# A slot table for two attention layers: transposes and maxima moved in front of the value sums, the turning of sums one slot later

## The chip, the cores and the metric

The kernel runs on one core of one Trainium2 chip. The metric is the device time of one execution in microseconds (us), lower is better. A core has five engines with queues of their own: TensorE (PE in the profile; PEld is its loading of weights), VectorE (DVE), ScalarE (ACT), GpSimd (POOL) and SyncE (SP, which only issues DMAs here). Each engine takes its own instructions in order and waits on semaphores for the others.

## What is computed

Four layers follow each other, A, B, A, B, on 2048 rows of 512 numbers; each layer normalises its input and adds its output to it. A is a linear attention. B, which the change touches, is a causal softmax attention inside four segments of 512 rows, with 32 heads of width 16, plus a memory that carries sums of keys and values from segment to segment:

```python
def _B_ref(x, wq, wk, wv, wo, beta):
    ...
    for s in range(N):
        qs, ks, vs = q[:, :, s], k[:, :, s], v[:, :, s]
        logits = jnp.einsum("bhqd,bhkd->bhqk", qs, ks) * scale + mask
        p = _softmax(logits, axis=-1)
        a_dot = jnp.einsum("bhqk,bhkd->bhqd", p, vs)
        pq = phi(qs)
        num = jnp.einsum("bhld,bhde->bhle", pq, M)
        den = jnp.einsum("bhld,bhd->bhl", pq, z)[..., None] + 1e-6
        a_mem = num / den
        o = g * a_mem + (1.0 - g) * a_dot
        outs.append(o)
        pk = phi(ks)
        M = M + jnp.einsum("bhld,bhle->bhde", pk, vs)
        z = z + jnp.einsum("bhld->bhd", pk)
    o = (lambda x, *d: x.transpose(*d))(jnp.stack(outs, 2).reshape(B, H, S, Dh), 0, 2, 1, 3).reshape(B, S, D)
    return o @ wo

x = A_x
x = x + _A_ref(_layernorm(x, axis=-1), A_wqkv, A_w_phi, A_wo)
x = x + _B_ref(_layernorm(x, axis=-1), B_wq, B_wk, B_wv, B_wo, B_beta)
x = x + _A_ref(_layernorm(x, axis=-1), A_wqkv, A_w_phi, A_wo)
x = x + _B_ref(_layernorm(x, axis=-1), B_wq, B_wk, B_wv, B_wo, B_beta)
```

## The kernel before

**Groups, rows and slots.** A layer B is 4 segments (s) of 8 groups (m counts all 32); a group is four heads. `LayerB.steps` (L1381) walks through slots k; R = 5 slots make a *row*, and row n of a segment holds the softmax of one group. In this document "slot 0" to "slot 4" are the five slots of a row (k % 5), and row 0 to row 7 the eight rows of a segment. Each layer has 160 such slots, after a lead-in of 25.

**What a slot issues, in this order** (L1470 to L1506): the group's logits and their exponentials (`attend`, L1193: TensorE writes tile `lg`, ScalarE takes the exponential into `P`, GpSimd cuts the diagonal blocks); one of five steps of the maxima of a later group (`maxima`, L1148: logits once more, into a pair of PSUM banks, and VectorE takes row maxima of them, the `top` operations, into `mxs`); work that was put off from earlier slots; `stack` (L1137: three DMAs on SP that put the split queries or keys, tile `ta`, into the stacked set `e`, when k % 5 is in `STACK`); the words of the slot's cell in the table that begin with `<`; in slot 0 the value sums of the group before (`weighted`, L1235: `P` times `v`, then ScalarE copies the sums to `U`); and then the other words of the cell.

**The order is fixed.** Every matmul and transpose passes through `held` (L165), and the other engines through `Ordered` (L145): each instruction of an engine stands behind the one before it in program order. So the table decides what each engine does next.

**The words** (`do`, L1395): `Q`, `V`, `O`, `P` with a number of steps are projections (TensorE, accumulating in `g` banks over four slots of a row); `a` is half of a memory read (`reads`, L1091); `t` and `m` are the two halves of a memory write (`writes`, L1106: `t` transposes keys on TensorE and ScalarE copies them to `KN`, `m` multiplies them with `v` and VectorE and GpSimd update the memory); `ln` is the transposing step of a later segment's normalisation (`columns`, L386: TensorE transposes, ScalarE writes `hh`, VectorE the rest `hl`), `n` and `N` are its earlier steps; `turn` (L1296) prepares the output rows of the segment before (with TensorE transposes only in the first segment, where the rows are those of layer A); `max` is `put_maxima` (L1184); `fin` is `finish` (L1261: VectorE turns `U` over, divides, and GpSimd adds to `ot`); `cv` is `convert` (L1286: VectorE turns finished sums `ot` for the output projection).

**PSUM.** Eight banks: two for `lg`, one each for `mx` and `my`, four for `g`. The maxima use `mx` and `my`, or two `g` banks where k % 5 is in `SPARE` (2, 4). `put_maxima` also uses `mx`:

```python
# maxima, L1172
if self.k % R in SPARE if self.k >= 0 else self.k % 2:
    pb = [PS("g", G) for _ in range(2)]
else:
    pb = [PS(t, 1) for t in ("mx", "my")]
# put_maxima, L1187
pt = PS("mx", 1)
tp(pt[0:16, 0:P], self.mx.pop(m), ident)
mt = T2("mt", MT, F32R, shape=(16, P))
act.activation(mt, pt[0:16, 0:P], AF.Copy, scale=-1.0)
```

`PS("mx", 1)` asks for a tile in the one buffer of that name; a new tile there waits until the tile before it has been read. The five steps of the maxima differ in width: in one step each bank takes 128 and 384 columns (twice, for two halves of the heads), in two steps 512, in one 256 twice.

**Lead.** The maxima of group m run in slots 5m - `LEAD` to 5m - `LEAD` + 4, and `max` in slot 0 of row n takes group n + 1. With `LEAD` = 9 the last of the five steps falls into that same slot 0.

**Projections to stacks.** `proj_pair` (L1035) ends in slot 4 of a row; `projected` (L1058) copies the result to `raw`, and in the next row splits it into `ta` (high part on ScalarE, low part on GpSimd): the queries in slot 1, the keys in slot 2. `stack` in row n takes group n + 3. The pairs stand in rows 0, 1, 4 and 6, so that three of the eight groups are stacked in the row in which they are split: those of rows 1, 5 and 7.

## Time and profile before

| | before |
|---|---|
| median of 3 runs | 1359.47 us (1357.38 to 1362.27) |
| the profiled execution, own time | 1360.54 us |
| its span, first to last instruction | 1358.8 us |
| mean granted TensorE clock | 0.994 |
| VectorE busy | 1045.2 us (77%) |
| ScalarE busy | 841.5 us (62%) |
| GpSimd busy | 751.4 us (55%) |

The first layer B lies at about 286 to 690 us of the span, the second at about 950 to 1340 us. A row takes some 12 to 13.5 us there. Busy TensorE time is modelled: a matmul's row in the trace runs from its start to the end of its drain, so that neighbouring rows overlap, and a wait shorter than the drain shows as no idle time of PE, but as idle time of PEld, which normally runs about a matmul ahead.

### The profile page before, as it was taken

The page shows a single profiled execution, that of the slowest core. Times are in us where ns is not written, and L with a number is a line of the kernel's source. Part 1 is how long each engine was busy: PE and PEld are TensorE (multiplying, and loading weights), DVE is VectorE, ACT ScalarE, POOL GpSimd, SP SyncE. Part 2 cuts the span into 40 slices and gives each one's busy share as a digit, 9 for nine tenths or more (in the row PEclk, how much of TensorE's full clock was granted, in tenths as well). Part 3 has the DMA queues.
Part 4 walks back from the last instruction along what each step waited for, and adds up shares of the span by engine and source line. Part 5 has one row for each costly group of instructions (what it writes and reads, how often), then busy time and mean ns, then how long its engine had stood idle before and what let it go on. Part 6 is the DMA issues. An engine that isn't in the chain of part 4 may idle for free.

```text
span 1358.8 us, 41839 instructions
## 1 busy us (share of the span) xinstructions
PE 1295.2 (95%) x16552; PEld 990.1 (73%) x16552; DVE 1045.2 (77%) x3247; ACT 841.5 (62%) x1274; POOL 751.4 (55%) x1116
## 2 busy tenths in 40 slices
PE   7999989999999999999999998999999999999987
PEld 6887868777767767767668886786777777777665
DVE  4766778778888888887767676787778789788785
ACT  5556345647777777676644433454677867867654
POOL 1668766225558668556324455551456667666552
PEclk9999999999999999999999998999999999999999
DMA  6398437534554545546350103745456454444432
GB/s 205 102 339 264 159 129 232 176 104 133 168 168 137 152 120 139 149 123 182 99 192 22 60 32 126 230 156 151 138 155 178 139 148 124 138 138 104 111 88 79
DMA packets 134419, 196.58 MB, mean 145 GB/s; under 512 B 15440, under 2 KB 61648, under 8 KB 133456
## 3 DMA queue, kind: packets, MB, share of 16 engines
q1 hardware_dynamic: 132256, 193.27, 47.5%
q8 instruction: 131, 2.15, 0.7%
q10 hardware_dynamic: 1968, 0.64, 0.2%
q14 instruction: 64, 0.52, 0.1%
HBM read 101.05 MB, written 39.85 MB: 104 GB/s over the span
## 4 chain that ended last, share of the span: by engine, by line
PE 67%; DVE 14%; ACT 8%; POOL 4%; issue 3%; DMA 2%; SPq 1%; DVEq 0%; ACTq 0%; POOLq 0%
PE g L177 52%; PE lg L177 6%; ACT P L155 4%; PE mx L177 3%; PE g L181 3%; DVE U L155 2%; PE lg L181 2%; DVE g L155 2%; POOL P L155 1%; POOL tb L155 1%; ACT ta L155 1%; DVE mx L155 1%; DVE es L155 1%; PE my L177 1%; DVE hl L155 1%
## 5 line engine op out<-in xcount | busy, mean ns | idle before, releaser
L155 ACT ACTIVATE P<-lg 128x1024 f32<-128x1024 f32 x316 | 324.3, 1026 | 126.1 <-PE lg L177 104.6
L155 POOL TENSOR_SCALAR_AFFINE_SELECT P<-P 128x256 f32<-128x256 f32 (+1 forms) x448 | 191.3, 442 | 197.2 <-ACT P L155 194.6
L155 DVE CUSTOM_DVE_ANT_0 g<-g,mask 128x256 f32<-128x256 f32 (+3 forms) x392 | 190.6, 542 | 17.9 <-PE g L177 17.8
L177 PE MATMUL g<-hh,wqk 64*128 64x512 f32 (+1 forms) x960 | 182.3, 394 | 1.6 <-SPq L155 0.7
L155 DVE CUSTOM_DVE_ANT_0 mx<-mx,mask 128x512 f32<-128x512 f32 (+2 forms) x316 | 158.4, 501 | 24.3 <-PE my L177 22.3
L177 PE MATMUL g<-w,oh 64*128 64x512 f32 (+2 forms) x848 | 170.8, 382 | 2.6 <-ACT oh L155 2.6
L177 PE MATMUL lg<-e,e 64*128 64x512 f32 (+1 forms) x1010 | 151.3, 345 | 13.2 <-ACT P L155 12.6
L155 DVE CUSTOM_DVE_ANT_0 my<-my,mask 128x512 f32<-128x512 f32 (+2 forms) x316 | 163.8, 518 | 0.0
L177 PE MATMUL g<-P,v 128*32 128x128 f32 (+3 forms) x2064 | 152.7, 434 | 1.2 <-DVE mxs L155 0.9
L177 PE MATMUL g<-w,hh 64*128 64x512 f32 (+1 forms) x672 | 143.2, 395 | 2.2 <-ACT w L155 1.3
L155 DVE DVE_READ_ACCUMULATOR2_ANT mxs<- 128x1 f32 x1024 | 144.0, 141 | 0.0
L177 PEld LDWEIGHTS lg<-e,e 64*128 64x128 f32 x1010 | 96.5, 185 | 54.1 <-ACT P L155 31.6
L177 PEld LDWEIGHTS g<-w,oh 64*128 64x128 f32 (+1 forms) x848 | 103.8, 187 | 16.8 <-ACT oh L155 3.5
L177 PEld LDWEIGHTS g<-hh,wqk 64*128 64x128 f32 (+1 forms) x960 | 98.4, 185 | 20.9 <-ACT hh L155 2.0
L177 PE MATMUL g<-w,ol 64*128 64x512 f32 (+2 forms) x424 | 112.1, 377 | 0.5 <-DVE ol L155 0.5
L177 PEld LDWEIGHTS g<-P,v 128*32 128x32 f32 x2064 | 64.1, 110 | 66.1 <-issue 49.1
L177 PE MATMUL g<-hl,wqk 64*128 64x512 f32 (+1 forms) x480 | 101.4, 392 | 2.1 <-DVE hl L155 2.1
L155 ACT COPY tb<-g 128x512 f32<-128x512 f32 (+1 forms) x132 | 70.9, 574 | 45.9 <-PE g L177 44.1
L177 PEld LDWEIGHTS g<-w,hh 64*128 64x128 f32 (+1 forms) x672 | 83.8, 188 | 16.4 <-ACT w L155 1.6
L177 PE MATMUL mx<-e,e 63*128 63x384 f32 (+3 forms) x323 | 89.7, 340 | 6.3 <-ACT mt L155 4.7
L155 POOL TENSOR_TENSOR ot<-ot,wt 128x256 f32<-128x256 f32 x46 | 33.9, 738 | 101.8 <-DVE wt L155 101.8
L177 PE MATMUL g<-w,hl 64*128 64x512 f32 (+1 forms) x336 | 89.4, 393 | 0.0
(164 smaller groups left out, 2987.1 us busy)
## 6 DMA issues: line engine op xcount, KB each, us to landing
e<-ta SPq DMA_DIRECT2D x384, 128.0 KB
wqk<-wqk SPq DMA_DIRECT2D x128, 256.0 KB
x<-x SPq DMA_DIRECT2D x48, 256.0 KB
pq<-tb SPq DMA_DIRECT2D x24, 256.0 KB
tb<-pq SPq DMA_DIRECT2D x24, 256.0 KB
x<-xr SPq DMA_DIRECT2D x22, 256.0 KB
xr<-x SPq DMA_DIRECT2D x20, 256.0 KB
x<-in SPq DMA_DIRECT2D x16, 256.0 KB
```

Of the source, the lines that this page charges most:

```text
L155: i = f(*a, **k)
L177: return held(nc.tensor.matmul(*a, **k))
L181: return held(nc.tensor.transpose(*a))
```

## The change

Only the constants and the four tables change; no function does. `max`, `turn`, `t` and `ln` get a `<` and so stand in front of the value sums of slot 0, and in front of `a`, which had one already; `m` comes a row sooner where it followed `t` by a row, behind the sums; `fin` moves from slot 0 to slot 1 (except in row 6 of `LAST` and `FINAL`), and some `cv` move by one or two slots. `LEAD` = 10 lets the five steps of the maxima run in slots 0 to 4 of one row, and `STACK` = (1, 3) puts the stacking DMAs a slot sooner.

```diff
-STACK = (2, 4)
+STACK = (1, 3)
 SPARE = (2, 4)
...
-LEAD = 9
+LEAD = 10
...
 FIRST = """
-0.0 max v3 fin | 0.1 Q2/6           | 0.2 Q2/6          | 0.3 Q2/6 | 0.4 Q2/6
-1.0 max t0 turn fin | 1.1 Q3/6      | 1.2 Q3/6          | 1.3 Q3/6 | 1.4 Q3/6
-2.0 m0 max turn t1 fin ln | 2.1 O/6 | 2.2 O/6           | 2.3 O/6 | 2.4 O/6
-3.0 m1 max turn turn fin ln | 3.1 O/6 | 3.2 O/6         | 3.3 O/6 | 3.4 O/6
-4.0 max ln ln fin | 4.1 Q0+/6 cv0   | 4.2 Q0+/6         | 4.3 Q0+/6 cv1 | 4.4 load Q0+/6
-5.0 max t2 fin | 5.1 V+/6           | 5.2 V+/6 n        | 5.3 V+/6 n | 5.4 V+/6 w
-6.0 m2 max t3 fin | 6.1 Q1+/6 cv2   | 6.2 Q1+/6 n       | 6.3 Q1+/6 n | 6.4 Q1+/6 w
-7.0 <a0+ m3 max fin | 7.1 V+/6 w | 7.2 V+/6 n        | 7.3 V+/6 n | 7.4 V+/6 w
+0.0 <max v3 | 0.1 Q2/6              | 0.2 Q2/6          | 0.3 Q2/6 | 0.4 Q2/6
+1.0 <t0 <turn <max m0 | 1.1 fin Q3/6 | 1.2 Q3/6         | 1.3 Q3/6 | 1.4 Q3/6
+2.0 <ln <t1 <turn <max m1 | 2.1 fin O/6 | 2.2 O/6       | 2.3 O/6 | 2.4 O/6
+3.0 <ln <turn <turn <max | 3.1 fin O/6 | 3.2 O/6        | 3.3 O/6 | 3.4 O/6
+4.0 <ln <ln <max | 4.1 fin Q0+/6    | 4.2 Q0+/6 cv0     | 4.3 Q0+/6 cv1 | 4.4 load Q0+/6
+5.0 <t2 <max m2 | 5.1 fin V+/6      | 5.2 V+/6 n        | 5.3 V+/6 n | 5.4 V+/6 w
+6.0 <t3 <max m3 | 6.1 fin Q1+/6     | 6.2 Q1+/6 n       | 6.3 Q1+/6 n cv2 | 6.4 Q1+/6 w
+7.0 <max <a0+ | 7.1 fin V+/6 w      | 7.2 V+/6 n        | 7.3 V+/6 n | 7.4 V+/6 w
 """
 GAPS = """
-0.0 <a0 max fin | 0.1 Q2/6 n cv3    | 0.2 Q2/6 n        | 0.3 Q2/6 n | 0.4 Q2/6
-1.0 <a1 max t0 turn fin | 1.1 Q3/6      | 1.2 Q3/6 n        | 1.3 Q3/6 | 1.4 Q3/6
-2.0 <a1 m0 max turn t1 fin ln | 2.1 O/6    | 2.2 O/6           | 2.3 O/6 | 2.4 O/6
-3.0 <a2 m1 max turn turn fin ln | 3.1 O/6  | 3.2 O/6           | 3.3 O/6 | 3.4 O/6
-4.0 <a2 max ln ln fin | 4.1 Q0+/6 cv0  | 4.2 Q0+/6       | 4.3 Q0+/6 cv1 | 4.4 load begin Q0+/6
-5.0 <a3 max t2 fin | 5.1 V+/6 | 5.2 V+/6 n N      | 5.3 V+/6 n N | 5.4 V+/6
-6.0 <a3 m2 max t3 fin | 6.1 Q1+/6 cv2   | 6.2 Q1+/6 n N     | 6.3 Q1+/6 n N | 6.4 Q1+/6
-7.0 <a0+ m3 max fin | 7.1 V+/6      | 7.2 V+/6 n N      | 7.3 V+/6 n N | 7.4 V+/6
+0.0 <max <a0 | 0.1 fin Q2/6 n       | 0.2 Q2/6 n        | 0.3 Q2/6 n cv3 | 0.4 Q2/6
+1.0 <t0 <turn <max <a1 m0 | 1.1 fin Q3/6 | 1.2 Q3/6 n   | 1.3 Q3/6 | 1.4 Q3/6
+2.0 <ln <t1 <turn <max <a1 m1 | 2.1 fin O/6 | 2.2 O/6   | 2.3 O/6 | 2.4 O/6
+3.0 <ln <turn <turn <max <a2 | 3.1 fin O/6 | 3.2 O/6    | 3.3 O/6 | 3.4 O/6
+4.0 <ln <ln <max <a2 | 4.1 fin Q0+/6 | 4.2 Q0+/6 cv0    | 4.3 Q0+/6 cv1 | 4.4 load begin Q0+/6
+5.0 <t2 <max <a3 m2 | 5.1 fin V+/6 | 5.2 V+/6 n N       | 5.3 V+/6 n N | 5.4 V+/6
+6.0 <t3 <max <a3 m3 | 6.1 fin Q1+/6 | 6.2 Q1+/6 n N     | 6.3 Q1+/6 n N cv2 | 6.4 Q1+/6
+7.0 <max <a0+ | 7.1 fin V+/6      | 7.2 V+/6 n N        | 7.3 V+/6 n N | 7.4 V+/6
 """
 LAST = """
-0.0 <a0 max fin | 0.1 Q2/6 n cv3    | 0.2 Q2/6 n        | 0.3 Q2/6 n | 0.4 Q2/6
...
-6.0 <a3 max fin pre | 6.1 cv2         | 6.2 P/4           | 6.3 P/9 | 6.4 P/5 v/1
-7.0 max fin | 7.1 P/4           | 7.2 P/5 v/1       | 7.3 P/4 v/1 | 7.4 P/5 v/2
+0.0 <max <a0 | 0.1 fin Q2/6 n       | 0.2 Q2/6 n        | 0.3 Q2/6 n cv3 | 0.4 Q2/6
+1.0 <turn <max <a1 | 1.1 fin Q3/6   | 1.2 Q3/6 n        | 1.3 Q3/6 | 1.4 Q3/6
+2.0 <ln <turn <max <a1 | 2.1 fin O/6 | 2.2 O/6          | 2.3 O/6 | 2.4 O/6
+3.0 <ln <turn <turn <max <a2 | 3.1 fin O/6 | 3.2 O/6    | 3.3 O/6 | 3.4 O/6
+4.0 <ln <ln <max <a2 | 4.1 fin v/2  | 4.2 v/2 cv0       | 4.3 v/2 cv1 | 4.4 v/2
+5.0 <max <a3 | 5.1 fin v/2          | 5.2 v/2           | 5.3 v/2 | 5.4 v/2
+6.0 <max <a3 fin pre | 6.1 cv2      | 6.2 P/4           | 6.3 P/9 | 6.4 P/5 v/1
+7.0 <max | 7.1 fin P/4              | 7.2 P/5 v/1       | 7.3 P/4 v/1 | 7.4 P/5 v/2
 """
 FINAL = """
-0.0 <a0 max fin | 0.1 Q2/6 cv3      | 0.2 Q2/6          | 0.3 Q2/6 | 0.4 Q2/6
...
-4.0 <a2 max turn turn fin | 4.1 O/6 cv1    | 4.2 O/6           | 4.3 O/6 | 4.4 O/6
...
+0.0 <max <a0 | 0.1 fin Q2/6         | 0.2 Q2/6          | 0.3 Q2/6 cv3 | 0.4 Q2/6
+1.0 <turn <turn <max <a1 | 1.1 fin Q3/6 | 1.2 Q3/6      | 1.3 Q3/6 | 1.4 Q3/6
+2.0 <max <a1 | 2.1 fin O/6          | 2.2 O/6 cv0       | 2.3 O/6 | 2.4 O/6
+3.0 <max <a2 | 3.1 fin O/6          | 3.2 O/6           | 3.3 O/6 | 3.4 O/6
+4.0 <turn <turn <max <a2 | 4.1 fin O/6 | 4.2 O/6        | 4.3 O/6 cv1 | 4.4 O/6
+5.0 <max <a3 | 5.1 fin O/6          | 5.2 O/6           | 5.3 O/6 | 5.4 O/6
+6.0 <max <a3 fin pre | 6.1 cv2      | 6.2 P/4           | 6.3 P/9 | 6.4 P/5
+7.0 <max | 7.1 fin P/4              | 7.2 P/5           | 7.3 P/4 | 7.4
 """
```

`FIRST` is the table of segment 0, `GAPS` of segments 1 and 2; segment 3 uses `LAST` in the first layer B and `FINAL` in the second.

## The prediction

> **What bounds the kernel now.** First the page's busy times, then a window in the first layer B (columns: us, then busy us and instructions of PE, PEld, DVE, ACT, POOL, the granted clock, DMA share, GB/s).

> ```profile
> PE 1295.2 (95%) x16552; PEld 990.1 (73%) x16552; DVE 1045.2 (77%) x3247; ACT 841.5 (62%) x1274; POOL 751.4 (55%) x1116
> ```

> ```profile
> 400.00:450.00 50.00, 48.71 (x752) 36.55 (x744) 40.38 (x150) 37.24 (x57) 34.33 (x52) 1.00 0.47 131
> ```

> TensorE is the bound, in the middle of layer B too: 48.7 of 50 us, with VectorE at 40.4 close behind. What a reordering can win is only what TensorE waits. The waits of its weight loads tell more than those of its matmuls, whose drains hide short stalls:

> ```profile
> PEld lg L177 <- ACT P L155: 31.6, 54, 1.8
> PEld g L177 <- DVE mxs L155: 22.9, 51, 1.3
> ...
> PEld mx L177 <- ACT mt L155: 13.6, 33, 0.6
> PEld g L177 <- POOL P L155: 13.1, 41, 0.8
> PEld g L177 <- DVE hl L155: 9.7, 14, 0.9
> ```

> Columns: total us, times, longest. Loads run about 0.2 us ahead (one weight load takes 0.19), so I count each such wait less 0.2 us as lost time.

> Now one slot 0 (a row 1 of `GAPS`) on TensorE, from the timeline:

> ```profile
> 411.45 0.39 PE L177 MATMUL lg<-e,e 64*128 64x512 f32 x2
> 411.68 0.39 PE L177 MATMUL mx<-e,e 63*128 63x512 f32 x1
> 412.00 0.77 PE L177 MATMUL g<-mem,tb 128*32 128x34 f32 x64
> 412.69 2.36 PE L177 MATMUL g<-P,v 128*32 128x512 f32 x32
> ...
> 415.27 0.28 PE L181 MATMUL mx<-ident,mxs 128*16 128x128 f32 x1
> 415.39 0.60 PE L181 MATMUL g<-ident,tb 128*128 128x128 f32 x4
> 415.82 0.60 PE L181 MATMUL g<-ident,x 128*128 128x128 f32 x4
> 416.35 0.50 PE L177 MATMUL lg<-e,e 64*128 64x512 f32 x2
> ```

> Logits, the maxima's products into mx and my, memory read (0.7 us), value sums, and only then, 3.6 us after the products, the turning of the maxima into the same bank mx. By then VectorE has long read mx, so this turning waits for nothing. That distance is what the change takes away.

> **The turned maxima, moved forward.** After it, slot 0 puts the 128- and 384-column step into mx and my, and `max` asks for bank mx with at most some transposes between. How long mx stays taken is seen where the same step stands today, in a slot 3:

> ```profile
> 407.44 0.28 PE L177 MATMUL mx<-e,e 63*128 63x256 f32 x1
> ...
> 407.73 0.40 PE L177 MATMUL g<-hh,wqk 64*128 64x512 f32 x2
> ...
> 407.93 0.30 DVE L155 CUSTOM_DVE_ANT_0 mx<-mx,mask 128x128 f32<-128x128 f32 x1 [0.33 <-PE my L177]
> ...
> 408.14 0.14 DVE L155 DVE_READ_ACCUMULATOR2_ANT mxs<- 128x1 f32 x1
> ...
> 408.91 0.14 DVE L155 DVE_READ_ACCUMULATOR2_ANT mxs<- 128x1 f32 x1
> ...
> 409.42 0.14 DVE L155 DVE_READ_ACCUMULATOR2_ANT mxs<- 128x1 f32 x1
> ```

> The third read, the last of mx, ends at 409.05, 1.61 us after the products began. TensorE learns of such an end 0.10 us later (below, 411.76 + 0.14 to 412.00). Its next work started 0.29 us after the products. So the wait is 1.61 + 0.10 - 0.29 = 1.42 us, less what stands between. A block of four transposes covers 0.43 us (415.39 to 415.82).

> ```profile
> 411.76 0.14 DVE L155 DVE_READ_ACCUMULATOR2_ANT mxs<- 128x1 f32 x1
> 412.00 0.66 PEld L177 LDWEIGHTS g<-mem,tb 128*32 128x32 f32 x64 [0.36 <-DVE mxs L155]
> ```

> So a row costs 1.42, 0.99, 0.56 or 0.13 us with 0, 1, 2 or 3 blocks in front of `max`. Blocks per row, from the tables: `GAPS` 0,1,2,1,2,1,1,0: 2 x 1.42 + 4 x 0.99 + 2 x 0.56 = 7.9 us, four such segments 31.7. `FIRST` (its `turn` transposes too) 0,2,3,3,2,1,1,0: 2 x 1.42 + 2 x 0.99 + 2 x 0.56 + 2 x 0.13 = 6.2, twice 12.4. `LAST` 0,0,1,1,2,0 in rows 0 to 5 (row 6 has no maxima beside it): 6.8. `FINAL` has none: 6 x 1.42 = 8.5. **Sum +59 us** in 60 rows. Behind the waiting turn stand, on TensorE, the read, the value sums and all later slots; nothing can pass it. Bounds: if the turn waited only for its own 128 columns (first read, ending at 408.28), a bare row costs 0.84 + 0.10 - 0.29 = 0.65, a row with one block 0.22, others nothing: 2 x 0.65 + 4 x 0.22 = 2.2 a `GAPS`, 19 in all. If for all four reads (409.56), 1.93: 0.51 x 60 = 31 more. I take 1.42, since the whole tile is handed on.

> VectorE can be late as well: normalisation steps stand in slots 3 and 4 of rows 5 and 6 of five segments. They already push its maxima late at 465.18, and I take +4 us (0 to 10).

> ```profile
> 464.36 0.69 DVE L155 BATCH_NORM_STATS2 bs<-x 128x6 f32<-128x512 f32 x1
> ...
> 465.18 0.67 DVE L155 CUSTOM_DVE_ANT_0 mx<-mx,mask 128x512 f32<-128x512 f32 x1
> ```

> **Stacking and LEAD.** The first products of a group move from slot 1 to slot 0, across the value sums. Their data come late in the three rows that split and stack at once:

> ```profile
> 405.24 0.46 PE L177 MATMUL lg<-e,e 64*128 64x256 f32 x4
> 407.91 0.60 ACT L155 CAST ta<-tb 128x512 fp32r<-128x512 f32 x1
> 408.60 1.28 POOL L155 TENSOR_TENSOR ta<-tb,ta 128x512 fp32r<-128x512 f32 x1 [0.68 <-ACT ta L155]
> 409.43 1.82 SPq L155 DMA_DIRECT2D e<-ta  x3
> ```

> The keys' low part is ready at 409.88 on GpSimd, and STACK = 3 cannot change that: the first DMA goes sooner, the second waits for it, and the third (0.6 us each) starts at about 410.5. How long one takes shows where a stack DMA is alone on the engines:

> ```profile
> 418.66 4.42 SPq L155 DMA_DIRECT2D e<-ta  x4
> ```

> ```profile
> 419.60:419.80 0.20, 0.20 (x4) 0.18 (x2) 0.20 (x1) 0.20 (x1) 0.20 (x1) 1.00 0.00 0
> 419.80:420.20 0.40, 0.40 (x6) 0.31 (x6) 0.40 (x3) 0.40 (x2) 0.34 (x2) 1.00 0.76 189
> 420.20:420.60 0.40, 0.40 (x9) 0.36 (x6) 0.40 (x2) 0.37 (x2) 0.40 (x2) 1.00 0.59 133
> ```

> Issued at 418.66, its bytes move from 419.8 to 420.6: 2.0 us. The third then lands at 412.5 or a little later; the products want it at 411.68, today only behind the logits of 416.35. That is 0.9 us, in rows 2 and 6 and the next row 0: 4 + 3 + 3 a layer, 20 rows, **+18 us** (bounds: 0 if the wait is absorbed, 2.0 us a row, 40, if SP's order delays it by a transfer). SP also holds the weight DMAs of slots 3 and 4 behind the stack now; they have the whole next slot 0 with its value sums to land in, so I cost them at nothing; without that cover each would cost up to a transfer, 2 us.

> **What it saves.** The turned maxima's copy `mt` no longer stands behind the copy of the sums `U` on ScalarE; slot 1's products find mx free:

> ```profile
> 390.68 0.18 PEld L177 LDWEIGHTS mx<-e,e 63*128 63x128 f32 x1 [0.62 <-ACT mt L155]
> ```

> `hl` no longer stands behind a `fin` that waits for `U`; and the longer slot 0 swallows the waits for a `g` bank and for `P`. The four rows: 22.9 + 13.6 + 13.1 + 9.7 = 59.3 us, less 0.2 x 139 = 27.8: **-31**. Of the waits for ScalarE's exponential (31.6 - 0.2 x 54 = 20.8) most arise in slots 2 and 3, from a slot 2 that holds an exponential, two activations and a cast; I take a quarter, **-5**. `fin` and `cv` later cost nothing: VectorE turns `U` behind slot 1's maxima instead of waiting for it, GpSimd's addition to `ot` now follows the split of `ta` instead of standing ahead of it, and the sums' next user is a row away; were that cover gone, a `fin` would cost TensorE nothing before an output projection waits. `m` sooner is the same work in the same slot 0.

> **Sum:** 59 + 4 + 18 - 31 - 5 = +45 us on the profiled execution's 1360.5 (span 1358.8 and 1.7 around it; the median of the runs is 1.1 less): 1405 us, **slower by 3.3%**.

> **The rivals.** *The turn waits only for its own columns, and the stacks land in time:* 19 + 4 - 36 = -13, **1347 us**, faster. It decides from the point where a bare row's wait falls under about 0.8 us (59 x 0.8 / 1.42 = 33, less than the 36 saved). For it: the first read ends early. Against: the bank mx is one tile, read by two operations. With the stack wait beside it, +5: **1366**, or within 0.3% when the savings are a little larger. *The stacks land in time,* all else as forecast: 1405 - 18 = **1387**. *The TensorE clock sinks with the new gaps:*

> ```profile
> 1290.43 0.50 PE L177 MATMUL lg<-e,e 64*128 64x256 f32 x4 [1.57 <-ACT P L155]
> ```

> ```profile
> 1292.00:1294.00 2.00, 1.61 (x32) 1.03 (x36) 2.00 (x11) 1.60 (x4) 1.92 (x2) 0.54 0.05 14
> 1294.00:1296.00 2.00, 2.00 (x65) 1.00 (x60) 1.93 (x7) 0.02 (x1) 2.00 (x4) 0.61 0.02 4
> ```

> After one gap of 1.57 us the granted clock was 0.54 and 0.61 for 4 us: 2 x 0.46 + 2 x 0.39 = 1.7 us lost. Rows with a gap of 1.4 us or more would be 21 bare ones and 14 more with the stack wait; if half trip it, 17 x 1.7 = 29: **1434**. [...]

> **Chances and range.** Forecast 0.56; stacks in time 0.15; clock 0.12; own columns 0.10, of which a little within; undecided near no change 0.07. Slower by over 0.3% 0.84, within 0.3% (about what a measurement of this kernel can tell from no change) 0.05, faster 0.11. The range runs from 1374 (a cheaper wait with stacks in time) to 1438 (the clock): it leaves out the faster cases and the 31 us of a wait for all four reads on top.

> **What would show it.** A new row of waits of PE or PEld at `mx L181` for `DVE mxs`, some 50 times, about 1 us each; waits of `mx L177` on the DMA `e<-ta`, some 20 times; `mx L177 <- ACT mt` nearly gone, and VectorE's waits for `U`; the exponential's waits of slot 3 still there. If `mx L181` waits under 0.7 us each, the forecast is wrong; if the span falls with those waits present, other stalls were larger than PEld's rows tell.

## The result, and the profile after

| | before | after |
|---|---|---|
| median of the runs made together | 1360.10 us (1357.38 to 1362.27, 4 runs) | 1453.37 us (1449.35 to 1455.30, 4 runs) |
| ratio, 95% interval | | 1.0683 (1.0652 to 1.0714) |
| the profiled execution, own time (span) | 1360.54 us (1358.8) | 1454.32 us (1452.6) |
| mean granted TensorE clock | 0.994 | 0.983 |

The changed kernel is 93 us slower, 6.8%. The forecast had the side right (slower) and the size wrong: 45 us, with a range that ended at 1438.

The page's busy times after, to set against those in the prediction: TensorE has the same 16552 matmuls and is a smaller share of a longer span.

```profile
PE 1308.4 (90%) x16552; PEld 997.1 (69%) x16552; DVE 1051.4 (72%) x3247; ACT 846.7 (58%) x1274; POOL 753.9 (52%) x1116
```

Where the 93 us are: windows over the layers B, first of before, then of after (columns as in the prediction: length, busy us of PE, PEld, DVE, ACT, POOL, the granted clock, DMA share, GB/s).

```profile
285.00:690.00 405.00, 392.53 (x5623) 290.06 (x5619) 327.12 (x1223) 292.05 (x432) 239.34 (x399) 1.00 0.50 142
949.00:1340.00 391.00, 373.41 (x5523) 275.79 (x5523) 316.26 (x1195) 280.59 (x417) 235.25 (x388) 1.00 0.47 131
```

```profile
285.00:735.00 450.00, 396.73 (x5606) 292.27 (x5602) 329.50 (x1221) 294.42 (x432) 240.13 (x399) 0.98 0.45 127
992.00:1432.00 440.00, 380.50 (x5515) 279.78 (x5515) 319.07 (x1196) 281.39 (x415) 235.39 (x386) 0.97 0.41 116
```

The layers B take 450 + 440 us in place of 405 + 391: +94, all of the difference. The busy times of VectorE, ScalarE and GpSimd there stay within 6 us of what they were; TensorE's grows by 11 us, at a granted clock of 0.98 and 0.97 in place of 1.00. The rest of the new time is waiting.

To see in which slot, I took from the timeline the start of the first logits matmul (`lg<-e,e`) of every slot and added up the distances by k % 5, over 31 rows of each layer B (us, both layers together):

| | slot 0 | slot 1 | slot 2 | slot 3 | slot 4 |
|---|---|---|---|---|---|
| before | 262.2 | 139.0 | 124.2 | 139.4 | 122.1 |
| after | 354.9 | 120.6 | 160.2 | 123.6 | 124.1 |
| difference | +92.7 | -18.4 | +36.0 | -15.8 | +2.0 |

Two slots lose, two win. A little of this is work that changed its slot: with `LEAD` = 10 slot 0 and slot 2 take a maxima step of 128 and 384 columns, which holds TensorE for some 0.29 us, and slot 1 and slot 3 one of 512 or of 256 twice (0.23 to 0.24 us); before, the wider step stood in slots 1 and 3. Over 61 rows that is some 4 us more in each of slots 0 and 2 and as much less in each of slots 1 and 3. The waits of TensorE in the changed kernel (total us, times, longest) name the two losses:

```profile
PE mx L181 <- DVE mxs L155: 63.3, 57, 3.0
PE g L177 <- SPq L155: 35.1, 28, 1.7
PE lg L177 <- ACT P L155: 8.3, 21, 1.3
...
PE mx L177 <- DMA e<-ta: 1.8, 1, 1.8
```

The first is the forecast wait of the turned maxima: 57 times, 1.11 us each. The second is not in the prediction: matmuls of the projections wait for SP's queue. In the profile before, this row is next to nothing:

```profile
PE g L177 <- SPq L155: 0.7, 2, 0.5
```

In the changed kernel 30.5 us of it, 21 waits, stand in slot 2. The wait for the stacks' landing, which the prediction put at 18 us, is one wait of 1.8 us.

The waits of the weight loads after, beside the four rows of the prediction whose 59.3 us were to be saved, and the exponential's:

```profile
PEld lg L177 <- ACT P L155: 17.0, 31, 1.6
...
PEld g L177 <- POOL P L155: 5.5, 17, 0.6
...
PEld g L177 <- DVE mxs L155: 1.9, 4, 0.8
...
PEld mx L177 <- ACT mt L155: 1.1, 2, 0.5
```

VectorE's waits for `U`, first before, then after: 50 became 6.

```profile
DVE U L155 <- ACT U L155: 53.9, 50, 3.9
```

```profile
DVE U L155 <- ACT U L155: 14.1, 6, 3.7
```

Two slots 0 without a transpose in front of `max`, in the timeline after: that of row 7 of the first segment, which has a normalisation step on VectorE beside it, and that of the next row 0.

```profile
380.33 0.28 PE L177 MATMUL mx<-e,e 63*128 63x256 f32 x1
...
381.45 0.69 DVE L155 BATCH_NORM_STATS2 bs<-x 128x6 f32<-128x512 f32 x1
...
383.44 0.14 DVE L155 DVE_READ_ACCUMULATOR2_ANT mxs<- 128x1 f32 x1
...
383.73 0.30 PE L181 MATMUL mx<-ident,mxs 128*16 128x128 f32 x1 [2.94 <-DVE mxs L155]
...
384.88 3.49 PE L177 MATMUL g<-P,v 128*32 128x512 f32 x32
...
398.57 0.35 PE L177 MATMUL mx<-e,e 63*128 63x256 f32 x1 [0.27 <-issue]
...
400.12 0.14 DVE L155 DVE_READ_ACCUMULATOR2_ANT mxs<- 128x1 f32 x1
...
400.41 0.27 PE L181 MATMUL mx<-ident,mxs 128*16 128x128 f32 x1 [1.28 <-DVE mxs L155]
...
401.36 3.79 PE L177 MATMUL g<-P,v 128*32 128x512 f32 x31
```

At 400.41 the turn waits 1.28 us (1.42 was worked out). It starts 0.15 us after the third read, the last of `mx`, has ended (400.12 + 0.14), as the prediction assumed. At 383.73, where VectorE comes to `mx` late, after the step before and the normalisation, it waits 2.94 us. Both times the value sums behind it are slow, 3.5 and 3.8 us instead of the 2.36 quoted in the prediction. The windows say why, by the granted clock, the third number from the end:

```profile
384.00:386.00 2.00, 2.00 (x73) 1.26 (x76) 0.86 (x5) 0.27 (x1) 0.00 (x0) 0.50 0.34 123
...
402.00:404.00 2.00, 2.00 (x20) 0.91 (x16) 0.51 (x2) 0.00 (x0) 1.21 (x1) 0.50 0.00 0
```

The trace has 10 such stretches inside the layers B (nine of 3.41 us and one of 6.83, at half clock), the kernel before has one there.

And the other loss, a slot 2 of a row that splits and stacks at once (row 5):

```profile
477.14 0.61 ACT L155 CAST ta<-tb 128x512 fp32r<-128x512 f32 x1
...
477.77 1.88 SPq L155 DMA_DIRECT2D e<-ta  x3
477.83 1.27 POOL L155 TENSOR_TENSOR ta<-tb,ta 128x512 fp32r<-128x512 f32 x1
...
479.76 0.51 PE L177 MATMUL g<-w,hh 64*128 64x512 f32 x2 [1.44 <-SPq L155]
```

SP issues three stacking DMAs from 477.77 to 479.65; one of them waits for GpSimd's low part, which ends at 479.10. TensorE's next projection matmul starts 0.11 us after SP is done. Why TensorE should wait for SP stands in the code (`mm3_pair`, L450): the two row halves of a pair take turns at a bank, and the turn is handed over by an empty instruction on SP, `passed = sync.nop(nofuse=True)`, which waits for the last matmul of one part and which the first matmul of the next part waits for. So SP does not only issue DMAs, as the list of the engines at the start of this document has it. In a row with such a projection, the hand-overs are issued at the end of slot 1 and at the end of slot 3. `STACK = (2, 4)` put the stacking DMAs behind them on SP's queue, `STACK = (1, 3)` puts them in front.

### The profile page after: what moved, and what is told of

Its sections match the earlier page's. It is cut to its first block, busy times and chain, and to the rows that moved or that the text cites. A ratio compares the mean times of both kernels' runs of the same rounds, so it can differ in the third digit from the quotient of the medians.

```text
span 1452.6 us, 41885 instructions
## 1 busy us (share of the span) xinstructions
PE 1308.4 (90%) x16552; PEld 997.1 (69%) x16552; DVE 1051.4 (72%) x3247; ACT 846.7 (58%) x1274; POOL 753.9 (52%) x1116
## 4 chain that ended last, share of the span: by engine, by line
PE 59%; DVE 20%; ACT 6%; issue 5%; POOL 4%; DMA 3%; SPq 2%; ACTq 1%; DVEq 0%; POOLq 0%
PE g L177 48%; PE lg L177 4%; DVE mx L155 4%; DVE g L155 4%; PE mx L177 2%; DVE my L155 2%; POOL ta L155 2%; DVE mxs L155 2%; ACT P L155 2%; DVE U L155 2%; SPq L155 2%; PE g L181 2%; PE lg L181 1%; ACT ta L155 1%; PE my L177 1%
## 5 line engine op out<-in xcount | busy, mean ns | idle before, releaser
L155 ACT ACTIVATE P<-lg 128x1024 f32<-128x1024 f32 x316 | 324.9, 1028 | 134.9 <-PE lg L177 103.0
L155 POOL TENSOR_SCALAR_AFFINE_SELECT P<-P 128x256 f32<-128x256 f32 (+1 forms) x448 | 192.3, 443 | 311.4 <-ACT P L155 306.9
L155 DVE CUSTOM_DVE_ANT_0 mx<-mx,mask 128x512 f32<-128x512 f32 (+2 forms) x316 | 158.3, 501 | 130.8 <-PE my L177 117.1
L177 PE MATMUL g<-hh,wqk 64*128 64x512 f32 (+1 forms) x960 | 182.9, 395 | 15.8 <-SPq L155 15.8
L155 DVE CUSTOM_DVE_ANT_0 g<-g,mask 128x128 f32<-128x128 f32 (+3 forms) x392 | 189.0, 536 | 9.4 <-PE g L177 8.9
L177 PE MATMUL g<-w,oh 64*128 64x512 f32 (+2 forms) x848 | 161.9, 379 | 3.3 <-ACT oh L155 2.6
L177 PE MATMUL g<-P,v 128*32 128x128 f32 (+3 forms) x2064 | 164.6, 461 | 0.0
L177 PE MATMUL g<-w,hh 64*128 64x512 f32 (+1 forms) x672 | 145.5, 402 | 20.6 <-SPq L155 18.6
L155 DVE CUSTOM_DVE_ANT_0 my<-my,mask 128x512 f32<-128x512 f32 (+2 forms) x316 | 163.6, 518 | 0.1
L177 PE MATMUL lg<-e,e 64*128 64x512 f32 (+1 forms) x1010 | 143.6, 340 | 9.2 <-ACT P L155 8.3
L155 DVE DVE_READ_ACCUMULATOR2_ANT mxs<- 128x1 f32 x1024 | 142.4, 139 | 0.0
L177 PEld LDWEIGHTS lg<-e,e 64*128 64x128 f32 x1010 | 93.5, 185 | 51.9 <-issue 17.4
L155 ACT ACTIVATE U<-g,share 128x512 f32<-128x512 f32 (+1 forms) x65 | 44.4, 683 | 138.9 <-PE g L177 138.7
L177 PEld LDWEIGHTS g<-hh,wqk 64*128 64x128 f32 (+1 forms) x960 | 97.5, 185 | 39.0 <-SPq L155 20.5
L177 PEld LDWEIGHTS g<-P,v 128*32 128x32 f32 x2064 | 68.9, 116 | 69.0 <-issue 60.1
L177 PEld LDWEIGHTS g<-w,hh 64*128 64x128 f32 (+1 forms) x672 | 82.3, 188 | 40.9 <-SPq L155 23.2
L177 PEld LDWEIGHTS g<-w,oh 64*128 64x128 f32 (+1 forms) x848 | 94.8, 186 | 20.2 <-ACT oh L155 3.5
L177 PE MATMUL g<-w,ol 64*128 64x512 f32 (+2 forms) x424 | 101.7, 377 | 0.5 <-DVE ol L155 0.5
L177 PE MATMUL g<-hl,wqk 64*128 64x512 f32 (+1 forms) x480 | 100.5, 390 | 0.0
L155 ACT COPY tb<-g 128x512 f32<-128x512 f32 (+1 forms) x132 | 70.9, 574 | 39.8 <-PE g L177 39.5
L177 PE MATMUL g<-w,hl 64*128 64x512 f32 (+1 forms) x336 | 89.5, 395 | 0.0
L155 DVE TENSOR_REDUCE es<-P 128x64 f32<-128x1024 f32 x64 | 77.4, 1209 | 13.2 <-ACT P L155 13.2
```

Of the source, the lines that this page charges most:

```text
L155: i = f(*a, **k)
L177: return held(nc.tensor.matmul(*a, **k))
```

## The experiments

All kernels are the one before or the changed one with the edit shown. Slot sums are those of the table above.

**1. The stacks alone.** Before, with one line changed:

```diff
-STACK = (2, 4)
+STACK = (1, 3)
```

> The kernel before with STACK = (1, 3) alone. Theory (SP): the three stacking DMAs wait on SP for the split part, and the hand-over between the halves of the rows in a pair of projections goes through SP too, so TensorE stands in slot 2 of rows 1, 5 and 7 (a pair and a fresh stack in one row) by 1.8 us: 19 rows, 34 us, of which some 8 to 12 are taken back in slot 3, where ScalarE was late anyway: 1378 to 1395 us, with a wait of PE g for SPq of 25 us or more. Rival (VectorE): slot 2 stands because fin was moved into slot 1; then 1360 us, within 4, and no wait for SPq. The recorded prediction, which priced an earlier stack at nothing on SP, also says 1360.

Measured 1400.79 us (1394.59 to 1404.78), ratio 1.0307 (1.0277 to 1.0337): +43 us from this line alone, somewhat above the expected range. Slot 2 goes from 124.2 to 171.7 us, 45.6 of these 47.5 us in rows 1, 5 and 7. A row 1 in its timeline:

```profile
408.70 0.60 ACT L155 CAST ta<-tb 128x512 fp32r<-128x512 f32 x1
...
409.32 2.41 SPq L155 DMA_DIRECT2D e<-ta  x3
...
409.90 1.28 POOL L155 TENSOR_TENSOR ta<-tb,ta 128x512 fp32r<-128x512 f32 x1
...
411.84 0.50 PE L177 MATMUL g<-hh,wqk 64*128 64x512 f32 x2 [1.92 <-SPq L155]
```

and its waits of TensorE:

```profile
PE g L177 <- SPq L155: 38.1, 26, 2.0
```

**2. The order of two things on SP.** The same kernel, slots and engines, but the stacking DMAs issued behind the words of the slot, so behind the hand-over:

```diff
-                m = k // R + 3
-                if 2 <= m < N:
-                    for side_ in range(2):
-                        if k % R == STACK[side_]:
-                            self.stack(m, side_)
                 what, s = table.get(k, ((), 0))
...
                 for w in what:
                     if w[0] != "<":
                         do(w, s, k)
+                m = k // R + 3
+                if 2 <= m < N:
+                    for side_ in range(2):
+                        if k % R == STACK[side_]:
+                            self.stack(m, side_)
```

> The kernel before with STACK = (1, 3), and in each slot the stacking DMAs issued behind the slot's words, so behind the projections' hand-over on SP instead of in front of it; slots, engines, data and every other instruction are those of the run that moved the stacks alone (1400.8 us). Theory (the hand-over stands behind a stacking DMA that waits for GpSimd): slot 2 of rows 1, 5 and 7 goes back to 1.9 us, the waits of PE g L177 for SPq (38 us, 26 times) go, and the time is that of the kernel before: 1356 to 1363. Rival (stacking so soon costs by itself, by its data being late or by contention with the weight DMAs): 1385 or more, slot 2 at 3.7 us or above.

Measured 1360.19 us (1358.14 to 1362.58, 12 runs) beside 1360.68 of before: ratio 1.0001 (0.9990 to 1.0012). Slot 2 is back at 124.2 us. The same place in its timeline: the DMAs go out at 408.08, the low part still ends late (408.41 + 1.30), and TensorE has gone on at 408.27 without a wait.

```profile
408.08 2.18 SPq L155 DMA_DIRECT2D e<-ta  x3
...
408.27 0.40 PE L177 MATMUL g<-hh,wqk 64*128 64x512 f32 x2
...
408.41 1.30 POOL L155 TENSOR_TENSOR ta<-tb,ta 128x512 fp32r<-128x512 f32 x1
```

```profile
PE g L177 <- SPq L155: 0.5, 1, 0.5
```

So the 43 us are the place of the hand-over behind a DMA that waits (with the clock beside its waits: seven half-clock stretches in the layers B in experiment 1, none here; the mean granted clock of the two profiled runs was 0.988 and 0.997), and nothing else about sooner stacks. This pair is the clearest of the study.

**3. The queries' stack only, moved to slot 2** in the changed kernel:

```diff
-STACK = (1, 3)
+STACK = (2, 3)
```

> The changed kernel with the queries' stack back in slot 2, the keys' stack still in slot 3 (STACK = (2, 3)). Theory (SP): the queries' DMAs then stand behind the first hand-over of a pair instead of ahead of it; slot 2 of rows 1, 5 and 7 falls from 3.7 to about 1.95 us (19 rows, 34 us), the second hand-over may cost up to 1 us more in slot 4 or the keys may land up to 1 us later for slot 0: 1410 to 1440 us, wait of PE g for SPq under 15 us. Rival (VectorE, fin in slot 1): slot 2 stays, 1450 us.

Measured 1484.28 us (1478.38 to 1486.04), ratio 1.0894 (1.0864 to 1.0925): slower, not faster. Slot 2 is indeed back (123.6 us), but slot 4 rises from 124.1 to 193.5: now the DMAs of both sides stand in front of the second hand-over.

```profile
PE g L177 <- SPq L155: 57.6, 47, 3.0
```

The mechanism was right; that the stall would move to the next hand-over was missed.

**4. The stacks on ScalarE's queue,** from experiment 1:

```diff
-                dma(d["set"][side][j:P:4, 2 * hf : 2 * hf + 2, :].rearrange("p r x -> p (r x)"),
-                    part[64 * hf : 64 * hf + 64, :])
+                act.dma_start(out=d["set"][side][j:P:4, 2 * hf : 2 * hf + 2, :].rearrange("p r x -> p (r x)").bitcast(F32),
+                              in_=part[64 * hf : 64 * hf + 64, :].bitcast(F32))
```

> The kernel before with the stacking DMAs in slots 1 and 3, as in the run that moved them alone (1400.8 us), but issued from ScalarE's queue, so that the hand-over of the pair of projections has SP's queue to itself. Theory (the 43 us are the hand-over held behind a stacking DMA on SP): slot 2 of rows 1, 5 and 7 goes back to about 1.95 us, the waits of PE g L177 for SPq nearly go, and the time falls by at least 25 us, to 1358 to 1378; what may be left is ScalarE held for up to 1.3 us behind a DMA that waits for GpSimd's low part. Rival (sooner stacks cost by contention on the DMA engines or by the data's lateness itself): 1390 or more, slot 2 stays at 3.7 us or above.

Measured 1438.09 us (1436.95 to 1441.85), ratio 1.0585 (1.0567 to 1.0603), far off. TensorE's waits for SP's queue are gone, but slot 2 stands at 163.6 us and slot 4 at 146.8, from another wait:

```profile
PE lg L177 <- ACT P L155: 69.4, 89, 1.8
```

```profile
312.57 2.67 ACTq L155 DMA_DIRECT2D e<-ta  x3
...
315.28 1.02 ACT L155 ACTIVATE P<-lg 128x1024 f32<-128x1024 f32 x1 [1.75 <-DMA e<-ta]
```

ScalarE issues for 2.67 us, with the second of the three DMAs waiting for GpSimd's low part, and its exponential follows only then. On either queue the held DMA held the work behind it. By itself this run does not tell the theory of experiment 1 from its rival; experiment 2 does.

**5. LEAD alone,** in the kernel before:

```diff
-LEAD = 9
+LEAD = 10
```

> The kernel before with LEAD = 10 alone: the maxima start in slot 0, max still stands behind the sums, the stacks still in slots 2 and 4. Recorded prediction's step: the stacked keys land too late for slot 0 of rows 2, 6 and the next row 0, by 1 to 1.6 us, 20 rows: 20 to 32 us, less about 5 for waits it swallows: 1375 to 1390 us. Rival: the landing has slack enough, 1360 us within 4.

Measured 1535.75 us (1532.86 to 1542.78), ratio 1.1322 (1.1292 to 1.1352), +176 us, far more than expected. Slot 0 goes to 447.6 us:

```profile
PE mx L177 <- DMA e<-ta: 98.1, 47, 3.8
```

With the keys stacked in slot 4, their landing is late for slot 0 in most rows, not only in those that split and stack at once, and the clock is at half in 33 stretches of the run, 122 us (mean granted clock 0.961). With the stacks where they stood, maxima a slot sooner do not pay.

**6. The changed kernel with the stacks put back:**

```diff
-STACK = (1, 3)
+STACK = (2, 4)
```

> The changed kernel with STACK = (2, 4) again. Theory (SP): slot 2 falls from 3.7 to 1.9 us in rows 1, 5 and 7, some 36 us; but the stacks then land later against slot 0, where rows 2, 6 and 0 wait up to 1.5 us more (20 rows, up to 30 us): between 1415 and 1450 us, the wait of PE g for SPq under 8 us, waits of mx or my for the stack in its place. Rival (VectorE holds slot 2): slot 2 stays at 3.7 us and the time at 1450 or more.

Measured 1586.01 us (1583.31 to 1591.45), ratio 1.1680 (1.1652 to 1.1707). Slot 2 is back at 123.1 us, as expected, but the time is far outside the expected range, because slot 0 pays far more (523.4): the landing wait of experiment 5 on top of the turn's.

```profile
PE mx L177 <- DMA e<-ta: 91.6, 44, 3.9
PE mx L181 <- DVE mxs L155: 43.9, 52, 2.1
```

**7. `max` behind the value sums,** in the changed kernel; all else in front stays. One row of the tables stands for all of them:

```diff
-1.0 <t0 <turn <max <a1 m0 | 1.1 fin Q3/6 | 1.2 Q3/6 n   | 1.3 Q3/6 | 1.4 Q3/6
+1.0 <t0 <turn <a1 max m0 | 1.1 fin Q3/6 | 1.2 Q3/6 n   | 1.3 Q3/6 | 1.4 Q3/6
```

> The changed kernel with max behind the value sums again, all else as changed. Theory: the turn's wait for bank mx is 59 us or more of the change and the half-clock stretches (10 in the layers B, 1.7 us each) follow from it; 1453 less 60 to 80 and plus about 7 for the copy mt that stands behind U again: 1380 to 1400 us, no wait of mx L181 for DVE mxs, and two or three half-clock stretches at most. Rival (the turn only shows the wait, VectorE is late for another reason and the next instruction would wait as long): 1440 us or more.

Measured 1406.10 us (1405.12 to 1408.30), ratio 1.0352 (1.0337 to 1.0368): 47 us less than the changed kernel, 6 us above the expected range. Slot 0 falls from 354.9 to 285.9 us, slot 1 rises from 120.6 to 142.8, where the wait for the copy `mt` returns.

**8. The turned maxima in another bank,** in the changed kernel, `max` still in front:

```diff
-            pt = PS("mx", 1)
+            pt = PS("g", G)
```

> The changed kernel, but the turned maxima go into a g bank instead of mx; order and data as changed. Theory: the turn waits for bank mx, not for its data (the maxima of the group are complete a slot before): the wait of mx L181 for DVE mxs (63 us) goes, slot 0 of bare rows falls from 5.1 to about 3.8 us, and most of the ten half-clock stretches with it; rows with two or three transpose blocks may now wait for a g bank: 1390 to 1425 us. Rival (the data are late, VectorE is behind): the wait stays with the turn, 1440 us or more.

Measured 1405.25 us (1399.69 to 1407.72), ratio 1.0322 (1.0296 to 1.0348), as expected: 48 us less than the changed kernel, with the place of `max` untouched.

```profile
PE g L177 <- SPq L155: 36.8, 26, 2.6
PE g L181 <- DVE mxs L155: 9.6, 11, 1.3
```

So most of what the turn waited for was the bank `mx`, not its data; the wait for SP's queue is as in the changed kernel (35.1 us). The time is that of experiment 7: with `max` in front, in a `g` bank, the kernel is no faster than with `max` behind the sums, in `mx`.

**9. Both cures in the changed kernel:** the edits of 8 and of 4 together.

> The change with both causes taken away: the turned maxima in a g bank, and the stacking DMAs from ScalarE's queue. Theory (bank mx 47 us and SP's queue 43 us make up nearly the whole 93): 1353 to 1375, no waits of PE mx L181 for mxs, those of g L177 for SPq under 10 us, slot 2 at about 1.95 us. Rival (a third cause, such as the sooner maxima themselves): 1380 or more.

Measured 1549.57 us (1541.96 to 1557.77), ratio 1.1405 (1.1373 to 1.1436). The waits `mx L181` and `SPq` are gone as expected, but ScalarE's queue is no cure (experiment 4), and here the keys also land late:

```profile
PE lg L177 <- ACT P L155: 69.9, 101, 2.2
PE mx L177 <- DMA e<-ta: 37.4, 32, 3.2
```

A version of the change without both causes was therefore not made (the order of experiment 2 in the changed kernel was not run); that the two are nearly all of the 93 us rests on the sum of experiments 1 and 8.

**10. The front words without sooner stacks and maxima.** The tables of experiment 7, with `STACK = (2, 4)` and `LEAD = 9`; so `t`, `ln` and `turn` in front, `m` sooner, `fin` and `cv` later:

> Of the change only what does not touch bank mx or SP: ln, t and turn in front of the value sums, m in the earlier row, fin and cv later; LEAD = 9, STACK = (2, 4), max behind the sums. Theory: what is left are the savings (hl no longer behind fin, memory reads no longer first at the g banks, ScalarE less behind): 1360 less 8 to 25: 1335 to 1352 us. Rival (the recorded savings do not exist, or the front work itself costs: g banks taken before the value sums): 1358 us or more.

Measured 1374.24 us (1372.16 to 1377.93, 6 runs), ratio 1.0101 (1.0082 to 1.0121). The rival held: slot 0 takes 282.9 us against 262.2 of the kernel before, slot 1 146.5 against 139.0. The two waits shown were 4.7 and 4.9 us before.

```profile
PE mx L177 <- ACT mt L155: 11.6, 36, 0.5
PE g L177 <- DVE mxs L155: 10.8, 13, 1.3
```

**11. The same with the turned maxima in a `g` bank** (edit of 8):

> As e6_front_only, with the turned maxima in a g bank, so that slot 1's products find mx free of the copy mt (13.6 us of weight-load waits, 33 times, before): 3 to 9 us under e6_front_only. Rival: the g bank is then missing for the pair of projections in slot 1, and the time is that of e6_front_only or above.

Measured 1347.39 us (1346.61 to 1353.29, 6 runs), ratio 0.9912 (0.9891 to 0.9933), faster than the kernel before. The copy `mt` no longer holds slot 1 (124.9 us); the gain over experiment 10, 27 us, is larger than expected.

**12 and 13. Which part of 11 wins.** First only the bank (edit of 8 in the kernel before), then the bank and the later `fin` and `cv` of the change, with nothing in front; again one row for all:

```diff
-1.0 <a1 max t0 turn fin | 1.1 Q3/6      | 1.2 Q3/6 n        | 1.3 Q3/6 | 1.4 Q3/6
+1.0 <a1 max t0 turn | 1.1 fin Q3/6 | 1.2 Q3/6 n   | 1.3 Q3/6 | 1.4 Q3/6
```

> The kernel before; only the turned maxima take a g bank instead of mx. Theory: the 27 us between the two runs with front words came from ScalarE's copy mt and the read of mx that the next products wait for; here the kernel before has 13.6 us of PEld waits of mx for mt, so the waits of mx L177 for mt go and the time falls by 5 to 12 us: 1348 to 1355. Rival (one g bank less for the projections and the reads costs as much as it frees): 1357 to 1364.

> The same with the turning of the sums a slot later, as in the change, and cv with it; nothing stands in front of the value sums. The prediction cost this move at nothing, so: within 4 us of the run with the g bank alone. If the later turning is worth something (VectorE no longer waits for U), it is 4 to 10 us below that run; if it costs (VectorE's work for slot 1 and the memory's sums collide), it is as much above. Against 1347.4 of the run that also has t, ln and turn in front, it tells what the front words are worth: I expect 0 to 6 us.

The bank alone: 1354.43 us (1351.66 to 1355.09), ratio 0.9959 (0.9946 to 0.9973). With the later `fin`: 1345.24 us (1344.87 to 1347.77), ratio 0.9902 (0.9888 to 0.9915), the fastest kernel here, 1.0% under the one before. The intervals are apart, so turning the sums a slot later, with `cv`, is worth 9 us. It comes from slot 3 (142.8 to 133.0) and slot 2 (124.3 to 119.6), less 7.7 us that slot 0 loses. The exponential's waits, bank alone first:

```profile
PEld lg L177 <- ACT P L155: 37.3, 59, 1.7
```

```profile
PEld lg L177 <- ACT P L155: 27.7, 45, 1.5
```

The front words of experiment 11 add nothing to it: 0.9912 against 0.9902, intervals that overlap.

## Why the prediction was wrong in size

Its own steps, in its order:

- **TensorE's waits decide:** right. The 94 us in the layers B are waits and lost clock; the other engines' busy times hardly moved.
- **The turned maxima wait for bank `mx`, +59, and VectorE late, +4:** right. 63.3 us in 57 waits, 1.28 us in a bare row. That the total meets the 63 so closely is partly luck: most rows waited a little less than worked out, and five rows 7 waited 2.85 to 3.02 us, about 8 us for VectorE's lateness there in place of 4. Experiment 8 shows that it is the bank: in another one the same instruction at the same place waits 9.6 us in 11 waits. The rival "waits only for its own columns" is out. (The slot 0 shown at 411.45 is one of a row 2 of `GAPS`, not of a row 1; nothing rests on that.)
- **Stacks land late for slot 0, +18:** not seen, 1.8 us in one wait. The rival "stacks in time" was right in this. Experiments 5 and 6 show that the price itself was far too low where stacks are not sooner: over 90 us in 44 to 47 waits.
- **"SP also holds the weight DMAs of slots 3 and 4 behind the stack now ... so I cost them at nothing":** this step failed. It asked what stands behind the stacking DMAs on SP, and named only DMAs. Behind them stands the hand-over of `mm3_pair`, which TensorE waits for. Slot 2 of the changed kernel is 36 us longer, some 4 of them the wider maxima step; alone the hand-over cost +43 (experiment 1), and with the two in the other order nothing (experiment 2, 0.9990 to 1.0012).
- **Savings, -31 and -5:** the waits went, but the sum does not show it. Of the four rows of 59.3 us, 5.5 (`P`), 1.9 (`mxs`) and 1.1 (`mt`) are left, and `hl` has no row any more; experiment 12 gives the `mt` term by itself, 5 us of time. Slots 1 and 3 fell by 18.4 and 15.8, together -34, near the forecast -36 partly by luck. Some 8 of these are the narrower maxima steps; `LEAD` alone (experiment 5) takes 3.5 and 3.8 us off the two slots. Some 7 in slot 3 come back from the stall in slot 2: where slot 2 does not stand (experiment 3), slot 3 takes 130.3 us, not 123.6. And most of the waits for `mxs` and `P` (33 of 36 us) stood in slot 0, which rose. The exponential's waits, which were to stay in slot 3, mostly went (22.6 to 5.5 us there).
- **"`fin` and `cv` later cost nothing":** better than that. Experiment 13 against 12 gives -9 us, by the waits for the exponential. In the timeline before, GpSimd's low part of `ta` starts at 405.90, behind the addition to `ot` (404.83 + 0.74), 0.61 us after ScalarE's high part has ended; in the changed kernel's it starts at 477.83, 0.08 us after the high part, and the addition follows at 479.46. Whether this order alone brings the gain was not tried.
- **The clock rival, +29 where 17 rows trip:** it happened beside the forecast, smaller. Nine more stretches in the layers B, one of them double, are 34 us at half clock; at most half of that, 17 us, is lost. The clock stood at 0.50 from 402 to 404 us after gaps of 0.27 and 1.28 us, so also behind gaps shorter than the 1.4 us by which the rival picked its rows. Which of the 57 waits have a stretch beside them, the last section shows.

What the sum lacks is thus +36 for the hand-over and up to +17 of clock, less 16 for the stacks in time. With the 63 of the turn and the -34 of savings that gives 63 + 36 + 17 + 2 - 34 = 84 of the 94 us. Some 10 us, in slot 0, are left. About 4 are the wider maxima step. For the rest, experiment 10 shows a source that the sum had no term for: with the front words and the later `fin` alone, slot 0 is 20.7 us longer. How much of this the longer wait of the changed kernel covers stays open. Taken by experiments instead, the turn's place (47 to 48 us with its clock and its savings) and the stacks (43 with theirs) make 90 to 91 of 93.

## What to carry to other kernels

Before an instruction that may wait is moved on a queue, list everything that the queue carries, empty synchronising instructions too, and who waits for each: SP was taken for a queue of DMAs here, yet it handed TensorE from one half of a projection to the other. Work that needs no result may still need a buffer: a transpose moved close behind a product in the same single bank waited here until that bank had been read, 57 times, 63.3 us in all. Another bank gave back 48 us of time here, though no run here shows a gain from the move itself. When several moves belong together, try each by itself in both directions: here the later turning of the sums, together with the other bank, was worth 1.0%, and the rest of the change hid it.
